# Earlier start of the first attention tile, earlier settling of two experts, and one pool of PSUM banks, in a recurrent-attention and top-1 router kernel

## The chip, the core and the metric

The kernel runs on one core of one Trainium2 chip. The metric is the device time of one execution in microseconds (us), lower is better. The core has five engines that run their own instruction streams in order: PE (TensorE, matmuls and transposes, with its weight loads shown as PEld), DVE (VectorE), ACT (ScalarE), POOL (GpSimd) and SP (SyncE, which here issues most of the DMA transfers). A stream waits for another through semaphores, and an instruction that waits holds up everything behind it on its engine.

## The reference

The first part is a linear recurrence over a sequence, for 4 batches, 8 heads, 768 steps, 48 values a head. The second part is a router that sends each of the 3072 rows to one of 8 experts of two matmuls each.

```python
for t in range(S):                       # B, H, S, D = 4, 8, 768, 48
    cur = einsum('bhd,bhe->bhde', u * k_t, v_t)          # a step's own term
    y[:, :, t] = einsum('bhd,bhde->bhe', r_t, state + cur)
    state = w * state + einsum('bhd,bhe->bhde', k_t, v_t)
x = y as 3072 rows of 384
xn, en = x / |x|, expert_emb / |expert_emb|
logits = xn @ en.T / tau                 # 8 experts
e = argmax(logits); gate = softmax(logits)[e]
out[row] = gate * (relu(x[row] @ w1[e]) @ w2[e])         # w1 384x1024, w2 1024x384
```

All arithmetic is float32.

## The kernel before

**Attention.** The sequence is cut into 6 chunks of 128 steps. A unit is one chunk of one batch, so there are 24 units, taken batch by batch within a chunk, and the function `attention` runs one turn for each, `i` from -1 to 23. The order of all instructions is written out by hand (`tc.manual_schedule()`), and the engines take them in that order. Turn `i` finishes unit `i` and prepares those after it:

- `load` (L262) fetches K, R and V of a unit in three transfers of 192 KB; turn `i` asks for unit `i+5`.
- `scaled` (L283) multiplies K by powers of the decay, and `own` (L287) computes u*K*R, a unit's own term. Both are on POOL; three instructions a unit. `own_sum` (L297, DVE) adds the own term up to eight numbers a step, `diag`, and `own_rows` (L303, ACT) multiplies V with them.
- `turn_r` and `turn_k` (L316, L327) transpose R and K on PE; their results are taken out of PSUM by DVE (`RT`) and ACT (`KT`). `scores` (L338) multiplies them, `masked` (L349, DVE) takes the scores out and cuts them to a triangle, in two halves `AT`, and `sums` (L382) multiplies these with V. `rows` (L416) turns the result into rows X, and `put` (L611, SP) writes them to DRAM as `xs`.
- every fourth turn the steps of the router run for the chunk that is complete: `logits`, `choose`, `before`, `ranks`, `places`, `exps`, `gates`, `lanes`, `listed`, `taken`, `summed`. They choose an expert for each row and build lists of which row takes which place at its expert.

`build_first` (L48) is the prologue: it computes the powers of the decay and prepares unit 0 up to its transposes. `build_consts` (L111) comes after it and makes masks and counters on POOL, and starts the ACT queue's loads of `u` (repeated over 128 partitions, 192 KB), `expert_emb`, `tau` and `w`. In turn -1 the own terms of units 0 and 1 are both computed, behind the scaling of unit 1. Three PE transposes of the expert embeddings (`build_experts`, L209) come at the top of turn 3, and some constants for the lists (`build_turned`, L169, DVE) at the end of turn 2.

**Two experts settled ahead.** After four of the six chunks, `settle` (L716) ranks the experts by the rows they have so far and settles which two are last in rank. Their first 128 rows each are then known, so that these two tiles (`Early`, L935) can be computed while the last two chunks are still being ranked. With `j = i - 12`:

```python
if j == 9:                                     # turn 21, before sums
    settle(k, load_, count)                    # DVE
    load_weights(k, expert_number(k, LAST[0]), k.weights[0])   # SP: w1, w2
    perm = turner(k, k.by)                     # DVE
if j == 10:                                    # turn 22, before sums
    k.lists = turned_lists(k, perm, "st")      # PE
    lists = taken_by_rank(k, k.lists)          # DVE
    first = [Early(k, r, *lists, w) for r, w in zip(LAST, k.weights)]   # POOL gathers
```

An expert's weights are 3 MB in two transfers. After the loop comes a passage written out by hand that ranks the last chunk and has the `Early` matmuls between its steps (`fill`).

**Experts.** `experts` (L1304) then runs eight blocks, one for each expert in the order `TURN`; each gathers its rows from `xs`, turns them (L1104), multiplies them with both weights, and scatters the result to `out` (L1020).

**PSUM.** It holds eight banks, and each tile here fills at most one. The attention part has a pool `aps` with two banks for each of the tags `tp`, `at` and `y` and one each for `st` and `xp`; this is closed at the end of the attention part, and the experts open a pool `ps` of eight.

Of the kernel before, what the change touches and what calls it, by code (L numbers as in the profile page):

```python
# [25 lines left out]
NK = DM // 128  # L26
# [21 lines left out]
def build_first(k):  # L48


    nc, pool = k.nc, k.aconst
    wc = pool.tile([128, NP], F32, name="wc")
    nc.vector.memset(wc, 1.0)
    with nc.allow_non_contiguous_dma(reason="384 words"):
        for s, q in ((0, nc.sync), (1, nc.scalar)):
            q.dma_start(out=wc[s * DP : s * DP + D, :], in_=k.w.rearrange("(p s) d -> s d p", s=2)[s])
    k.ones = k.const.tile([128, 128], F32, name="ones")
    nc.vector.memset(k.ones, 1.0)
    wide = k.work.tile([128, 512], F32, name="wide", tag="AT1")
    nc.vector.memset(wide, 1.0)  # L60
    k.ident = k.const.tile([128, 128], F32, name="ident")
    make_identity(nc, k.ident)

    ps = k.ps.tile([128, 512], F32, name="wake", tag="tp")
    for _ in range(WAKE):
        nc.tensor.matmul(ps, k.ones, wide, start=True, stop=True)
    for lst, name, count in ((k.Kpad, "Kpad", 4), (k.Rpad, "Rpad", AHEAD + 2)):
        for i in range(count):
            t = pool.tile([128, H, DP], F32, name=f"{name}{i}")
            nc.gpsimd.memset(t[:, :, D:DP], 0.0)  # L70
            lst.append(t)
    load(k, 0, nc.scalar)


    nc.vector.tensor_scalar(wc, wc, W_MIN, W_MAX, ALU.max, ALU.min)
    t = pool.tile([128, NP, C], F32, name="wpow")
    for p in range(NP):
        nc.vector.tensor_tensor_scan(
            t[:, p, :], wc[:, p : p + 1].to_broadcast([128, C]), k.ones, 1.0, ALU.mult, ALU.mult
        )  # L80
    mid = pool.tile([128, NP], F32, name="mid")
    nc.vector.reciprocal(mid, t[:, :, C // 2])
    over_i = mid[:, :, None].to_broadcast([128, NP, C])
    kp = k.work.tile([128, NP, C], F32, name="kp", tag="AT0")
    nc.vector.tensor_mul(kp, t[:, :, ::-1], over_i)
    ps = k.ps.tile([128, NP, 2, DP], F32, name="kpT", tag="xp")
    for p in range(NP):
        nc.tensor.transpose(ps[:, p].rearrange("q s d -> q (s d)"), kp[:, p, :], k.ident)
    k.rpow = pool.tile([128, NP, C], F32, name="rpow")
    nc.vector.tensor_mul(k.rpow, t, over_i)  # L90
    cols = ps[:, :, :, 0:D]
    nc.vector.tensor_mul(
        k.Kpad[0].rearrange("q (p s) d -> q p s d", s=2)[:, :, :, 0:D],
        k.loaded[0][0].rearrange("q (p s) d -> q p s d", s=2), cols,
    )
    turn_r(k, 0)
    k.kpow = pool.tile([128, H, D], F32, name="kpow")
    nc.vector.tensor_copy(k.kpow.rearrange("q (p s) d -> q p s d", s=2), cols)  # L98
    turn_k(k, 0)
    k.wC = t[:, :, C - 1 : C].to_broadcast([128, NP, D])  # L100
# [7 lines left out]
    return f  # L108


def build_consts(k):  # L111
    nc, pool = k.nc, k.const

    k.umask = pool.tile([128, 128], F32, name="umask")
    nc.gpsimd.memset(k.umask, 0.0)
    nc.gpsimd.affine_select(
        out=k.umask, in_=k.umask, compare_op=ALU.is_ge, fill=1.0,
        base=0, pattern=[[-1, 128]], channel_multiplier=1,
    )
    k.u_bc = k.aconst.tile([128, H, D], F32, name="u_bc")  # L120
    nc.scalar.dma_start(
        out=k.u_bc.rearrange("p h d -> p (h d)"),
# [7 lines left out]
    )  # L130
    k.wrow = k.aconst.tile([1, DM], F32, name="wrow")
    nc.scalar.dma_start(out=k.wrow, in_=k.w.rearrange("(o h) d -> o (h d)", o=1))
    k.yT = [k.aconst.tile([128, 2, NP // 2, C], F32, name=f"yT{i}") for i in range(2)]
    for b in range(B):
        t = k.aconst.tile([128, NP, D], F32, name=f"state{b}")
        nc.gpsimd.memset(t, 0.0)
        k.state.append(t)
    k.half = pool.tile([128, B], F32, name="half")
    nc.gpsimd.memset(k.half, 0.5)

# [68 lines left out]
def build_experts(k):  # L209

    nc, pool = k.nc, k.aconst
    emb, tau = k.emb_rows, k.tau_rows
    sq = k.work.tile([E, DM], F32, name="emb_sq", tag="sq")
    nrm = pool.tile([E, 1], F32, name="emb_nrm")
    nc.scalar.activation(sq, emb, ACT.Square, accum_out=nrm)
    nc.gpsimd.tensor_tensor(out=nrm, in0=nrm, in1=k.half[0:E, 0:1], op=ALU.pow)
    yield
    nc.vector.tensor_scalar_add(nrm, nrm, 1e-6)
    nc.vector.reciprocal(nrm, nrm)
    nc.vector.reciprocal(tau, tau)  # L220
    nc.vector.tensor_scalar(emb, emb, nrm, tau, ALU.mult, ALU.mult)
    yield
    ps = k.ps.tile([128, NK, E], F32, name="ps", tag="xp")
    for c in range(NK):
        nc.tensor.transpose(ps[:, c, :], emb[:, c * 128 : (c + 1) * 128], k.ident[0:E, 0:E])
    k.ent = k.const.tile([128, NK, 32], F32, name="ent")
    nc.vector.memset(k.ent, 0.0)
    nc.vector.tensor_copy(k.ent[:, :, 0:E], ps)
    yield

# [573 lines left out]
def attention(k):  # L804
# [17 lines left out]
    for i in range(-1, units):  # L822
        j = i - SETTLED * B
        if 0 < i + AHEAD < units:
            load(k, i + AHEAD)
        if 1 <= i < 4:
            next(emb)
        whole(summed, i - 6)
        whole(places, i - 4)
        whole(logits_out, i - 3)  # L830
        if i >= 0:
            on(turn_r, i + 1)
        if i < units - 1:
            on(own_rows, i, 0)
        if i >= 0:
            on(turn_k, i + 1)
        whole(turn_logits, i - 3)
        on(scaled, i + 2)
        for n in (0, 1) if i < 0 else (i + 2,):
            on(own, n)  # L840
        on(states, i)
        of_group(squares, i - 1)
        if i < units - 1:
            on(own_rows, i, 1)
        whole(norms, i - 2)
        whole(choose, i - 3)
        whole(before, i - 3)
        whole(located, i - 4)
        whole(gates, i - 5)
        whole(lanes, i - 5)  # L850
        whole(listed, i - 5)
        on(own_sum, i + 1)
        if j == 9:
            settle(k, load_, count)
            load_weights(k, expert_number(k, LAST[0]), k.weights[0])
            perm = turner(k, k.by)
        if i == units - 2:
            own_rows_once(k, i + 1)
        if j == 10:
            k.lists = turned_lists(k, perm, "st")  # L860
            lists = taken_by_rank(k, k.lists)
            first = [Early(k, r, *lists, w) for r, w in zip(LAST, k.weights)]
        on(sums, i)
        whole(exps, i - 4)
        on(carry, i)
        on(scores, i + 1)
        on(masked, i + 1, 0)
        on(rows, i)
        on(masked, i + 1, 1)
        of_group(put, i)  # L870
        of_group(turn_rows, i - 1)
        whole(logits, i - 2)
        whole(ranks, i - 3)
        whole(taken, i - 5)
        if i == B:
            decays(k)
        if i == 2:
            build_turned(k)
        if 3 <= i < 3 + len(k.ring):
            k.nc.gpsimd.memset(k.ring[i - 3], 0.0)  # L880
        if j == 7:
            load_, count = loads(k, "st")
        if j == 10:
            to = outs(k, lists[0], E * TM)

# [28 lines left out]
    exps(k, h)  # L914
    located(k, h)
    lanes(k, h)
    summed(k, g)
    by = order(k, load_, k.settled)
    perm = turner(k, by)
    gates(k, h)  # L920
    listed(k, h)
    fill(6)
    taken(k, h, "tp")
    summed(k, h)
# [508 lines left out]
def attention_pools(k, ctx):  # L1433
    for name, bufs in (("work", 2), ("rows", 3), ("rt", 2)):
        setattr(k, name, ctx.enter_context(k.tc.tile_pool(name=name, bufs=bufs)))
    k.ps = Banks(ctx.enter_context(k.tc.tile_pool(name="aps", bufs=1, space=PSUM)))


class Banks:


    def __init__(self, pool):
        self.pool = pool

    def tile(self, shape, dtype, name, tag):
        return self.pool.tile(shape, dtype, name=name, tag=tag, bufs={"tp": 2, "at": 2, "y": 2}.get(tag, 1))


def expert_pools(k, ctx):
    for name, bufs in (("gp", 8), ("xtp", 2), ("hp", 2)):  # L1450
        setattr(k, name, ctx.enter_context(k.tc.tile_pool(name=name, bufs=bufs)))
    k.ps = ctx.enter_context(k.tc.tile_pool(name="ps", bufs=8, space=PSUM))


@with_exitstack
def kernel(
# [23 lines left out]

    n.const = pool("const", 1)
    n.wp = pool("wp", 2)
    n.xs = tc.dram_tile([N, DM], F32, name="xs")
    n.list = tc.dram_tile([E, 128, TT], I32, name="list")
    n.tlist = tc.dram_tile([E, 128, TT], I32, name="tlist")
# [8 lines left out]
    with ExitStack() as ctx2, ExitStack() as ctx1, tc.manual_schedule():  # L1494
# [1 line left out]
        n.io = ctx1.enter_context(tc.tile_pool(name="io", bufs=AHEAD + 2))  # L1496
        attention_pools(n, ctx1)
        build_first(n)
        for i in range(1, AHEAD - 1):
            load(n, i)  # L1500
        build_consts(n)
        attention(n)
        ctx1.close()
        expert_pools(n, ctx2)
# [32 lines left out]
```

## Time and profile before

The time before is 424.53 us, the median of three runs from 424.11 to 425.92. The profiled execution has a span of 423.8 us.

| stage | us from the start | what bounds it in the profile |
|---|---|---|
| prologue and turn -1 | 0 to 12.3 | a chain over DVE, PE and POOL |
| wait of PE | 12.3 to 16.6 | no matmul runs |
| turns 0 to 23 | 16.6 to 146.7 | PE, with few gaps |
| wait of PE | 146.7 to 149.5 | no matmul runs |
| passage by hand | 149.5 to 178.2 | PE |
| experts | 178.2 to 412 | PE |
| last scatters | 412 to 423.8 | no matmul runs |

PE is busy for 398.1 us, DVE 251.6, ACT 171.4 and POOL 160.0. The transfers' queues move 54.39 MB. To read it: a gap on an engine other than PE matters only where PE waits for what comes behind it.

### The profile page before, as it was taken

The page shows a single profiled execution, that of the slowest core. Times are in us where ns is not written, and L with a number is a line of the kernel's source. Part 1 is how long each engine was busy: PE and PEld are TensorE (multiplying, and loading weights), DVE is VectorE, ACT ScalarE, POOL GpSimd, SP SyncE. Part 2 cuts the span into 40 slices and gives each one's busy share as a digit, 9 for nine tenths or more (in the row PEclk, how much of TensorE's full clock was granted, in tenths as well). Part 3 has the DMA queues.
Part 4 walks back from the last instruction along what each step waited for, and adds up shares of the span by engine and source line. Part 5 has one row for each costly group of instructions (what it writes and reads, how often), then busy time and mean ns, then how long its engine had stood idle before and what let it go on. Part 6 is the DMA issues. An engine that isn't in the chain of part 4 may idle for free.

```text
span 423.8 us, 9269 instructions
## 1 busy us (share of the span) xinstructions
PE 398.1 (94%) x3542; PEld 355.1 (84%) x3542; DVE 251.6 (59%) x608; ACT 171.4 (40%) x517; POOL 160.0 (38%) x217
## 2 busy tenths in 40 slices
PE   7599999999999789999999999999999999999980
PEld 4477888888888676689999999999999999799680
DVE  5377886867679755066765857175456456566310
ACT  1567776767677511233333233223233233223020
POOL 6777678686855215140140511140240240300210
PEclk9889999999999989999999999999999999999996
DMA  9977757666741982124643614164164160140101
GB/s 151 195 157 152 151 130 148 133 144 131 149 94 45 360 322 57 39 76 157 225 160 131 224 37 148 49 217 151 37 226 148 39 223 2 44 162 1 56 20 43
DMA packets 93800, 54.39 MB, mean 128 GB/s; under 512 B 76937, under 2 KB 88380, under 8 KB 93746
## 3 DMA queue, kind: packets, MB, share of 16 engines
q1 hardware_dynamic: 89024, 43.85, 38.9%
q0 software_dynamic: 3296, 9.44, 6.7%
q10 hardware_dynamic: 1426, 0.41, 0.5%
q8 instruction: 30, 0.49, 0.5%
q14 instruction: 24, 0.20, 0.2%
HBM read 44.45 MB, written 9.63 MB: 128 GB/s over the span
## 4 chain that ended last, share of the span: by engine, by line
PE 80%; POOL 6%; DMA 5%; issue 3%; DVE 2%; SPq 2%; ACT 0%; POOLq 0%; ACTq 0%
PE ps L1156 24%; PE ps L1220 15%; PE ps L1260 5%; PE at L345 4%; PE y L406 4%; PE ps L1273 4%; PE ps L1134 2%; PE ps L1104 2%; PE early_y L975 2%; PE y L397 2%; PE kt L333 2%; PE early_h L966 2%; PE st L366 2%; PE yrows L424 2%; PE rt L322 2%
## 5 line engine op out<-in xcount | busy, mean ns | idle before, releaser
L1020 POOL DMA_INDIRECT out_dram<-y,to x25 | 29.8, 1193 | 176.4 <-issue 118.6
L1156 PE MATMUL ps<-xTe,w 128*128 128x192 f32 (+3 forms) x336 | 63.0, 327 | 0.0
L1156 PEld LDWEIGHTS ps<-xTe,w 128*128 128x128 f32 x336 | 55.8, 190 | 0.6 <-ACT p L1170 0.2
L308 ACT ACTIVATE xd<-V,diag 128x48 f32<-128x48 f32 x184 | 46.2, 325 | 3.2 <-DVE diag L299 3.2
L351 DVE TENSOR_TENSOR AT<-at,umask 128x512 f32<-128x512 f32 x48 | 32.9, 686 | 22.1 <-PE at L345 22.1
L1163 ACT ACTIVATE hT<-hT 128x384 f32<-128x384 f32 (+3 forms) x42 | 21.9, 523 | 33.8 <-DVE hT L1186 15.4
L1220 PE MATMUL ps<-Tw,Sh 128*128 128x192 f32 x192 | 32.5, 326 | 0.0
L1220 PEld LDWEIGHTS ps<-Tw,Sh 128*128 128x128 f32 x192 | 31.4, 190 | 0.0
L406 PE MATMUL y<-AT,V 128*48 128x128 f32 (+1 forms) x384 | 26.9, 281 | 4.4 <-DVE AT L351 4.4
L345 PE MATMUL at<-RT,KT 48*128 48x128 f32 x384 | 28.8, 291 | 1.3 <-ACT KT L335 0.7
L1011 POOL DMA_INDIRECT G<-xs,take x25 | 26.2, 1048 | 9.8 <-issue 4.6
L1156 PE MATMUL ps<-Tx,Sw 128*128 128x192 f32 (+3 forms) x168 | 29.8, 327 | 0.0
L345 PEld LDWEIGHTS at<-RT,KT 48*128 48x128 f32 x384 | 24.1, 193 | 5.9 <-ACT xd L308 2.8
L1173 DVE TENSOR_TENSOR u<-ps,p 128x384 f32<-128x384 f32 (+3 forms) x14 | 7.8, 558 | 35.4 <-PE ps L1156 30.7
L1156 PEld LDWEIGHTS ps<-Tx,Sw 128*128 128x128 f32 x168 | 27.6, 190 | 0.2 <-DVE Tx L1287 0.2
L406 PEld LDWEIGHTS y<-AT,V 128*48 128x48 f32 (+1 forms) x384 | 20.5, 125 | 8.1 <-DVE AT L351 4.7
L512 ACT COPY xT<-xp 128x384 f32<-128x384 f32 x24 | 11.5, 478 | 34.1 <-PE xp L510 34.1
L292 POOL TENSOR_TENSOR KU<-K,u_bc 128x384 f32<-128x384 f32 x24 | 24.1, 1003 | 3.1 <-DMA K<-in_k_dram 3.1
L293 POOL TENSOR_TENSOR KU<-KU,Rpad 128x384 f32<-128x384 f32 x24 | 24.1, 1003 | 1.9
L284 POOL TENSOR_TENSOR Kpad<-K,kpow 128x384 f32<-128x384 f32 x23 | 23.0, 1001 | 2.9 <-DVE kpow L98 2.9
L1220 PE MATMUL ps<-w,hT 128*128 128x192 f32 x128 | 23.4, 326 | 0.0
L1220 PEld LDWEIGHTS ps<-w,hT 128*128 128x128 f32 x128 | 21.3, 190 | 0.3
(239 smaller groups left out, 806.0 us busy)
## 6 DMA issues: line engine op xcount, KB each, us to landing
w<-in_moe_w_dram SPq DMA_DIRECT2D x16, 1536.0 KB, 7.6
K<-in_k_dram SPq DMA_DIRECT2D x24, 192.0 KB, 3.0
V<-in_v_dram SPq DMA_DIRECT2D x24, 192.0 KB
xs<-X SPq DMA_DIRECT2D x24, 192.0 KB, 13.0
Rpad<-in_r_dram SPq DMA_DIRECT2D x23, 192.0 KB, 5.8
G<-xs,take POOLq DMA_INDIRECT x27
out_dram<-y,to POOLq DMA_INDIRECT x25
Rpad<-in_r_dram ACTq DMA_DIRECT2D x1, 192.0 KB
```

What stands on the lines that cost most here:

```text
L284: k.nc.gpsimd.tensor_mul(k.Kpad[i % len(k.Kpad)][:, :, 0:D], k.loaded[i][0], k.kpow)
L292: nc.gpsimd.tensor_mul(KU, K, k.u_bc)
L293: nc.gpsimd.tensor_mul(KU, KU, R[:, :, 0:D])
L308: k.nc.scalar.mul(k.xd[i][:, h, :], V[:, h, :], diag[:, h : h + 1])
L345: nc.tensor.matmul(at[s][:, p, :], KT[rows, p, :], RT[rows, p, :], start=True, stop=True)
L351: k.nc.vector.tensor_mul(a, k.at[i][s], k.umask[:, None, :].to_broadcast([128, NP, C]))
L406: mm(y[s][u * DP : u * DP + n, q, :], V[:, h * D : h * D + n], AT[s][:, p, :], start=(c == 0 and q == 0), stop=True, skip_group_check=True,)
L1011: nc.gpsimd.indirect_dma_start(out=G[0:n, :], out_offset=None, in_=k.xs[:, :], in_offset=IndirectOffsetOnAxis(ap=take[0:n], axis=0), bound ...
L1020: put = k.nc.gpsimd.indirect_dma_start(out=k.out[:, :], out_offset=IndirectOffsetOnAxis(ap=to, axis=0), in_=y, in_offset=None, bounds_chec ...
L1156: nc.tensor.matmul(ps[:, j, :], weights[:, (f + j) * 128 : (f + j + 1) * 128], moving, start=(first and j == 0), stop=True, skip_group_che ...
L1163: nc.scalar.activation(h, h, ACT.Relu)
L1220: nc.tensor.matmul(ps, a[:, f, :], b[:, f, :], start=(first and f == 0), stop=(f == NF // 2 - 1), skip_group_check=True)
```

## The change

The change has three parts. The first brings what unit 0's mask step waits for ahead: the small loads go out at the start on the ACT queue, the constants follow at once on POOL, and unit 0's own term is computed in the prologue. In turn 0 the second half of `own_rows` goes ahead of `turn_k`; the embedding's steps move behind `own_sum`, `build_turned` from turn 2 to turn 5, and the zeroing of `ent` from DVE to POOL. The second settles the two experts a turn sooner, with the gathers put ahead of the second weight transfer, and in the passage by hand it brings the last chunk's `gates` and `listed` ahead of the ordering. The third replaces both PSUM pools by one with eight named banks, of which each tag has its own and the experts' tag goes round all eight.

```diff
 build_first:
     load(k, 0, nc.scalar)
+    load(k, 1)
+    load_consts(k)          # u_bc, emb, tau, wrow on the ACT queue
+    build_consts(k)
+    for i in range(2, AHEAD - 1):
+        load(k, i)
+    own(k, 0)
 build_consts:
+    k.ent = pool.tile([128, NK, 32], F32, name="ent")
+    nc.gpsimd.memset(k.ent, 0.0)
 attention:
-        if 1 <= i < 4:
-            next(emb)
         whole(summed, i - 6)
...
+        if i == 0:
+            own_rows(k, i, 1)
         if i >= 0:
             on(turn_k, i + 1)
...
-        for n in (0, 1) if i < 0 else (i + 2,):
-            on(own, n)
+        on(own, i + 2)
...
-        if i < units - 1:
+        if 0 < i < units - 1:
             on(own_rows, i, 1)
...
         on(own_sum, i + 1)
-        if j == 9:
-            settle(k, load_, count)
-            load_weights(k, expert_number(k, LAST[0]), k.weights[0])
-            perm = turner(k, k.by)
+        if 1 <= i < 4:
+            next(emb)
+        if j == 7:
+            load_, count = loads(k, "xp")
         if i == units - 2:
             own_rows_once(k, i + 1)
-        if j == 10:
+        if j == 9:
+            perm = turner(k, k.by)
             k.lists = turned_lists(k, perm, "st")
             lists = taken_by_rank(k, k.lists)
             first = [Early(k, r, *lists, w) for r, w in zip(LAST, k.weights)]
+            load_w2(k, number, k.weights[0][1])
         on(sums, i)
...
-        if i == 2:
+        if i == B + 1:
             build_turned(k)
...
-        if j == 7:
-            load_, count = loads(k, "st")
+        if j == 8:
+            settle(k, load_, count)
+            number = expert_number(k, LAST[0])
+            load_w1(k, number, k.weights[0][0])
         if j == 10:
             to = outs(k, lists[0], E * TM)
 the passage by hand:
     lanes(k, h)
+    gates(k, h)
+    listed(k, h)
     summed(k, g)
     by = order(k, load_, k.settled)
     perm = turner(k, by)
-    gates(k, h)
-    listed(k, h)
     fill(6)
 PSUM:
-    k.ps = Banks(ctx.enter_context(k.tc.tile_pool(name="aps", bufs=1, space=PSUM)))
-    k.ps = ctx.enter_context(k.tc.tile_pool(name="ps", bufs=8, space=PSUM))
+    HELD = {"tp": (0, 1), "at": (2, 3), "y": (4, 5), "st": (6,), "xp": (7,), "ps": (0, 1, 6, 7, 2, 3, 4, 5)}
+    n.ps = Banks(pool("psum", 1, space=PSUM))
```

More of the change, by code (lines that the diff above doesn't have):

```diff
@@ L108, in numbers, with load_consts @@
     return f
[L111 to L119, printed above, removed]
+def load_consts(k):
+    nc = k.nc
     k.u_bc = k.aconst.tile([128, H, D], F32, name="u_bc")
@@ L132, in build_consts @@
     nc.scalar.dma_start(out=k.wrow, in_=k.w.rearrange("(o h) d -> o (h d)", o=1))
+def build_consts(k):
+    nc, pool = k.nc, k.const
+    k.umask = pool.tile([128, 128], F32, name="umask")
+    nc.gpsimd.memset(k.umask, 0.0)
+    nc.gpsimd.affine_select(
+        out=k.umask, in_=k.umask, compare_op=ALU.is_ge, fill=1.0,
+        base=0, pattern=[[-1, 128]], channel_multiplier=1,
+    )
     k.yT = [k.aconst.tile([128, 2, NP // 2, C], F32, name=f"yT{i}") for i in range(2)]
@@ L225, in build_experts @@
         nc.tensor.transpose(ps[:, c, :], emb[:, c * 128 : (c + 1) * 128], k.ident[0:E, 0:E])
-    k.ent = k.const.tile([128, NK, 32], F32, name="ent")
-    nc.vector.memset(k.ent, 0.0)
     nc.vector.tensor_copy(k.ent[:, :, 0:E], ps)
@@ L1435, in attention_pools @@
         setattr(k, name, ctx.enter_context(k.tc.tile_pool(name=name, bufs=bufs)))
-    k.ps = Banks(ctx.enter_context(k.tc.tile_pool(name="aps", bufs=1, space=PSUM)))
 class Banks:
+    HELD = {"tp": (0, 1), "at": (2, 3), "y": (4, 5), "st": (6,), "xp": (7,), "ps": (0, 1, 6, 7, 2, 3, 4, 5)}
     def __init__(self, pool):
         self.pool = pool
+        self.next = {tag: itertools.cycle(banks) for tag, banks in self.HELD.items()}
     def tile(self, shape, dtype, name, tag):
-        return self.pool.tile(shape, dtype, name=name, tag=tag, bufs={"tp": 2, "at": 2, "y": 2}.get(tag, 1))
+        return self.pool.tile(shape, dtype, name=name, tag=f"bank{next(self.next[tag])}")
 def expert_pools(k, ctx):
@@ L1498 @@
         build_first(n)
-        for i in range(1, AHEAD - 1):
-            load(n, i)
-        build_consts(n)
         attention(n)
```

## The prediction, made before the changed kernel had run

> **What bounds the kernel now.** I read the page first, then the waits of PE, the timeline of the first 42 us, the granted clock in short windows, and the timeline from 126 to 182 us.
>
> ```profile
> PE 398.1 (94%) x3542; PEld 355.1 (84%) x3542; DVE 251.6 (59%) x608; ACT 171.4 (40%) x517; POOL 160.0 (38%) x217
> PE   7599999999999789999999999999999999999980
> PEclk9889999999999989999999999999999999999996
> ```
>
> PE is busy for 94% of the span, so only its own gaps and slow spells can be won back. They lie in slices 0 to 2 and 13 to 14 (a slice is 10.6 us). The waits of PE name them (total, times, longest, in us):
>
> ```profile
> PE y L406 <- DVE AT L351: 4.4, 1, 4.4
> PE early_x L955 <- DMA G<-xs,take: 2.8, 1, 2.8
> ...
> PE ps L1104 <- ACT earlyy L978: 0.7, 1, 0.7
> ...
> PE at L345 <- ACT xd L308: 0.6, 1, 0.6
> PE ps L225 <- ACT xT L512: 0.6, 1, 0.6
> PE take L672 <- POOL what L653: 0.5, 1, 0.5
> ```
>
> Each of the six is touched by this change. The timeline of the start (start, length in us, engine, line, instruction) shows the first:
>
> ```profile
> 8.84 0.35 ACTq L121 DMA_DIRECT2D u_bc<-in_u_dram  x1
> ...
> 9.24 1.00 POOL L284 TENSOR_TENSOR Kpad<-K,kpow 128x384 f32<-128x384 f32 x1 [2.91 <-DVE kpow L98]
> ...
> 13.35 0.99 POOL L292 TENSOR_TENSOR KU<-K,u_bc 128x384 f32<-128x384 f32 x1 [3.11 <-DMA K<-in_k_dram]
> 14.41 0.99 POOL L293 TENSOR_TENSOR KU<-KU,Rpad 128x384 f32<-128x384 f32 x1
> ...
> 15.44 0.55 DVE L299 TENSOR_REDUCE diag<-KU 128x8 f32<-128x384 f32 x1 [6.28 <-POOL KU L293]
> 15.91 1.28 DVE L351 TENSOR_TENSOR AT<-at,umask 128x512 f32<-128x512 f32 x2
> ```
>
> The scores of unit 0 are ready at 10.6, but the mask L351 stands on DVE behind the sum L299, and this waits for the own term, which POOL begins at 13.35. The page puts that on K; but K of unit 0 had already been read at 7.53, so I take it for `u_bc`, sent at 8.84 behind the copy of KT on ACT.
>
> A wait costs a second time. Busy time in windows (PE, PEld, DVE, ACT, POOL, granted clock, DMA share, GB/s):
>
> ```profile
> 12.30:16.60 4.30, 0.00 (x0) 0.00 (x0) 1.16 (x3) 1.07 (x7) 3.10 (x4) 1.00 1.03 203
> ...
> 17.20:24.00 6.80, 6.80 (x56) 5.54 (x55) 4.21 (x8) 3.85 (x15) 6.64 (x9) 0.50 0.90 175
> 146.80:149.50 2.70, 0.00 (x0) 0.00 (x0) 0.70 (x4) 0.44 (x1) 0.00 (x0) 1.00 0.95 337
> ...
> 150.20:153.70 3.50, 3.50 (x35) 2.71 (x34) 1.81 (x4) 1.26 (x4) 1.10 (x3) 0.51 0.98 393
> ```
>
> After the wait of 4.3 us PE runs at half clock for 6.8 us, and after that of 2.8 us for 3.5. Sixteen `scores` matmuls take 2.08 us at 18.29 and 1.16 at 24.97.
>
> **What the Trainium skill says.** "TensorE: Matmul & The Clock Gate", Part 1, says that PE's clock is halved after an idle window of about 3.4 us, restored after a busy one, and that the windows run freely. The trace agrees: the half-clock spells last one and two windows (3.5 and 6.8). It also shows that the window need not be wholly idle, for 2.8 us sufficed. The same page, Part 2 (architectural detail), has DVE, ACT and POOL as strict first-in first-out, as the mask behind the sum shows. "Trainium Kernel Development and Optimization", Key Constraints, says that the transfers of the SP, ACT and POOL queues share 16 engines; here 203 GB/s moved while `u_bc` was on its way.
>
> **The start.** With `load_consts` in the prologue, `u_bc` goes out behind R of unit 0 on the ACT queue, at about 1.9 us. By the windows 0.3 MB had moved at 4.0 and 0.93 MB at 6.9 us; K, R and V of unit 0 and `u_bc` are 0.79 MB, so it lands at about 6.2. As a bound, in the trace of before it took 4.5 us (8.84 to 13.35), which gives 6.4. POOL ends its constants at 6.33, and the zeroing of `ent` adds some 0.15. The own term of unit 0 then runs from 6.5 to 8.5 (2 x 1.00), in an interval where POOL idled until 9.24. The sum L299 follows `kpow` at 9.16 and ends at 9.7, before the scores at 10.6, so the masks run from 10.6 to 11.9. PE reaches `sums` of unit 0 at 12.2 and does not wait: **-4.4 us**. No mostly idle window remains, so the half clock of 6.8 us goes too: half of 6.8, **-3.4**.
>
> Do the later steps keep pace? POOL, at 3.6 us a turn, has scaled unit 2 by 13.2, and PE wants it at 15.3. Doing 8 `own_rows` ahead of KT(1) costs ACT 2.0 us from 9.75, and KT(1) is out at 12.3, wanted at 13.2. Units 0 to 5 and `u_bc` are 3.7 MB, at 185 GB/s in by about 21.6; unit 5 is wanted on POOL in turn 3 at 23. After that a turn needs 0.77 MB, 3.9 us at 197 GB/s, against 4.7 or more of PE. So transfers hide, with 2 us to spare at unit 5. One loss: the square of the embeddings (0.5 + 0.2 us) now stands on ACT in turn 1 behind the second half of `own_rows` and ahead of the copy of y that `rows` needs: between 0 and 0.7, I take **+0.5**.
>
> **Turn 3.** The embedding's transposes waited 0.57 for the bank `xp`, and the scores waited 0.59 (35.63) because DVE had `build_turned` and the `ent` steps (2.2 us) ahead of RT. Moved behind `states`, the first goes. In turn 6, where `build_turned`'s 1.95 us now fall, PE has 3.4 us of work between the rows and the scores instead of 2.5, since the state matmuls (0.65) are there; DVE needs 2.6 for constants and RT. So the second goes as well: **-1.2**.
>
> **Settling a turn sooner.** What it removes is the wait for the gather: **-2.8**, and the half clock behind it, **-1.7** (half of 3.5). What it adds is a wait of PE in turn 21. In the trace of before the DVE steps stand without a gap: the second mask ends at 132.73, then `summed`, RT, `own_sum`, `settle` (134.09 to 135.9) and `turner`, and `perm` is ready at 136.27. The new order holds the same instructions, with `settle` first. But the list matmul, which in turn 22 found `perm` long ready, now stands on PE in turn 21 right before `sums`, where PE arrives at 133.35. Behind it on PE is everything: `sums`, the next scores, the masks on DVE that need them. So PE waits **+2.9** (136.27 - 133.35). If that falls into one free-running window, the clock halves once more: 0 or 1.7, I take the middle, **+0.85**.
>
> The gather itself then has room. It starts near 137.5 instead of 142.59, and took 6.9 us with both weights in transfer; so it is there at about 145 on the old time axis, while PE reaches `early_x` at 146.7 + 2.9 = 149.6. That the first weights go out 1.5 us sooner changes nothing, for their first use was at 152.5. The second expert's go out some 3 us later and are wanted at 166.5, with 3 MB at 390 GB/s taking 8. So the wait moves from turn 23 to turn 21 and the part nets **-0.75**.
>
> **The passage by hand.** With `gates` ahead of the ordering, `what` L653 comes over 1 us sooner, and PE's 0.54 before `take` goes: **-0.5**. The ordering comes later, but it is hidden by `early_y`.
>
> **One PSUM pool.** The experts' first tile now takes bank 0, idle by then, instead of waiting until the last `early_y` is out of its pool: **-0.7**. Within each part the rotation over banks is as before, two for each of three tags and eight for `ps`; nothing for it. The expert phase and the last 12 us, where POOL scatters, keep their length.
>
> Sum: -4.4 - 3.4 + 0.5 - 1.2 - 0.75 - 0.5 - 0.7 = -10.4, so 424.5 - 10.4 = **414.1 us**.
>
> **Rivals.**
> - *The list wait isn't there.* If DVE had slack that the trace hides, the new wait and its clock share fall away: 414.1 - 3.75 = 410.3. Against it: DVE stands without a gap from 132.65 to 137.9.
> - *The start gives part back to the transfers.* If u_bc or the loads of units 2 to 5 come some 2 to 4 us later than reckoned, PE waits in turns 1 to 3, and a half-clock window can follow: about 3.4 less gained, 417.5. For it: from 4 to 22 us the DMA share is near 1.
> - *Slower.* `own` of unit 0 now stands on POOL ahead of the scaling of unit 1, which PE's KT(1) needs before `sums` of unit 0. If `u_bc` lands at 13.3 again, that costs about 0.9 and wins nothing at the start; if the gather is also late as before, the transition costs 2.9 + 0.85 more. With -1.2 - 0.5 - 0.7 this is 424.5 + 2.3 = 426.8. Against it: `u_bc` now has only R ahead of it in its queue, where before the loads of units 2 and 3 were in transfer with it.
>
> **How the numbers follow.** Forecast 0.60, no list wait 0.11, part given back 0.17, slower 0.06, and 0.06 for losses of several parts at once that leave it near no change. The range takes the forecast with its unknown terms (clock after the list wait 0 to 1.7, `emb` 0 to 0.7, `u_bc` by 1 us), most of the second rival and the edge of the first: 410.5 to 419. Half a per cent is 2.1 us: faster 0.88, within 0.06, slower 0.06.
>
> **What would show it.** Right: PE's first `y` L406 near 12.2, granted clock 1.0 through 24 us, own term on POOL at 6.5 to 8.5; a PE wait of about 3 us at the list matmul, released by DVE `perm`; no wait at `early_x`; no wait at the first L1104. Wrong: `u_bc` after 8 us, PE waits for loads before 30 us, a gather still awaited near the end of the loop, or any change of the span from the first L1104 to the end (245.5 us now).

## The result, and the profile after

The changed kernel takes 420.38 us (median of four runs, 419.49 to 420.78), the kernel before 424.77 beside it (424.11 to 425.92): a ratio of 0.9891 with a 95% interval of 0.9863 to 0.9919. That is 4.4 us less where 10.4 were forecast, and the time lies above the range of 410.5 to 419. The profiled span went from 423.8 to 418.9 us.

The page of the changed kernel, in busy time and in 40 slices (10.5 us each):

```profile
PE 397.3 (95%) x3542; PEld 355.0 (85%) x3542; DVE 254.4 (61%) x607; ACT 172.3 (41%) x517; POOL 161.2 (38%) x218
PE   6999999999996999999999999999999999999980
PEclk9899999999997999999999999999999999999996
```

PE's busy time hardly fell, 398.1 to 397.3. A half clock makes busy time longer, so had the half-clock spells of before gone (10.3 us of them, 5.1 us of loss), busy time would be some 5 us less. It is 0.8 less: 4.1 of the 4.9 us came out of idle time. Counting from 0, two slices of the clock line, besides the last, where PE has nothing left to do, show where full clock was still missing: slice 1, where the start was to have none left, and slice 12.

The waits of PE of the changed kernel (total, times, longest, in us):

```profile
PE lists L772 <- DVE perm L766: 3.3, 1, 3.3
...
PE kpT L94 <- DVE kp L91: 1.0, 1, 1.0
PE kt L343 <- DVE Kpad L98: 0.7, 1, 0.7
...
PE kt L343 <- DVE X L440: 0.4, 1, 0.4
PE yrows L434 <- ACT yT L421: 0.3, 1, 0.3
...
PE take L682 <- POOL what L663: 0.2, 1, 0.2
```

Gone are the waits for the first mask (4.4), at `early_x` (2.8), at the experts' first bank (0.7) and both of turn 3; that before `take` is 0.2 instead of 0.5. The list matmul waits 3.3, where 2.9 had been foretold. So the list of waits looks as forecast, but for two of the prologue: 1.0 at `kpT`, which is new, and 0.7 instead of 0.2 for `Kpad`. The windows tell the rest (PE, PEld, DVE, ACT, POOL, granted clock, DMA share, GB/s); two of them overlap:

```profile
11.20:14.50 3.30, 3.30 (x33) 2.97 (x35) 2.70 (x5) 1.51 (x6) 3.22 (x4) 0.51 1.41 196
14.50:24.00 9.50, 8.76 (x123) 7.29 (x121) 5.74 (x11) 6.37 (x23) 7.60 (x10) 0.99 1.08 197
...
128.70:132.00 3.30, 0.00 (x0) 0.03 (x1) 2.98 (x14) 2.00 (x7) 1.39 (x2) 0.81 0.15 24
131.00:137.50 6.50, 5.50 (x50) 4.50 (x50) 1.30 (x8) 0.75 (x2) 2.29 (x2) 0.50 0.83 297
137.50:142.00 4.50, 4.50 (x76) 3.58 (x74) 3.72 (x12) 3.16 (x12) 0.00 (x0) 0.99 1.08 379
```

The wait for the lists is idle PE from 128.7 to 132.0. Behind it the clock stays at a half until 137.5; PE worked 5.5 us in that time. If all of that work went at half speed, half of it, 2.7 us, is loss; this is an estimate, and so is each loss below that is half of PE's work in a spell. There is a spell at a half from 11.2 to 14.5 as well, worth 1.65.

A third view puts a date on each loss: the start of the `scores` of a unit, and of the experts' first transposes (L1104, now L1117). "Again" is another profile of the same changed kernel.

| start, us | before | changed | again |
|---|---|---|---|
| scores of unit 0 | 9.47 | 10.03 | 9.69 |
| unit 1 | 18.29 | 15.22 | 13.28 |
| unit 4 | 35.63 | 29.82 | 27.91 |
| unit 7 | 52.21 | 46.40 | 44.49 |
| unit 8 | 57.63 | 52.57 | 50.66 |
| unit 20 | 125.13 | 120.38 | 118.47 |
| unit 21 | 129.79 | 125.04 | 123.13 |
| first expert transposes | 178.25 | 173.64 | 170.74 |
| end of the span | 423.8 | 418.9 | 416.6 |

By unit 4 the changed kernel is 5.81 us ahead (7.72 again); by unit 8, 5.06 (6.97); by unit 21, 4.75 (6.66). From unit 21 to the experts before took 48.46, changed 48.60 (47.61 again): the settling, the hand passage and the pool together won nothing, or 0.85. The experts take as long as before (245.3 after 245.5).

### The profile page after: what moved, and what is told of

Same layout as the page of the kernel before. It is cut to its first block, busy times and chain, and to the rows that moved or that the text cites. A ratio compares the mean times of both kernels' runs of the same rounds, so it can differ in the third digit from the quotient of the medians.

```text
span 418.9 us, 9283 instructions
## 1 busy us (share of the span) xinstructions
PE 397.3 (95%) x3542; PEld 355.0 (85%) x3542; DVE 254.4 (61%) x607; ACT 172.3 (41%) x517; POOL 161.2 (38%) x218
## 4 chain that ended last, share of the span: by engine, by line
PE 82%; DVE 5%; POOL 4%; issue 3%; DMA 1%; ACT 1%; POOLq 0%; SPq 0%; DVEq 0%; ACTq 0%
PE ps L1169 24%; PE ps L1233 16%; PE ps L1273 5%; PE at L355 5%; PE y L416 5%; PE ps L1286 4%; PE early_y L988 3%; PE ps L1147 2%; PE early_h L979 2%; PE kt L343 2%; PE ps L1117 2%; PE y L407 2%; PE yrows L434 2%; PE st L376 2%; PE rt L332 2%
## 5 line engine op out<-in xcount | busy, mean ns | idle before, releaser
L1024 POOL DMA_INDIRECT G<-xs,take x25 | 26.7, 1067 | 10.5 <-issue 4.3
L1196 ACT ACTIVATE hT<-ps 128x384 f32<-128x384 f32 (+3 forms) x14 | 6.9, 491 | 36.0 <-PE ps L1169 36.0
```

What stands on the lines that cost most here:

```text
L1024: nc.gpsimd.indirect_dma_start(out=G[0:n, :], out_offset=None, in_=k.xs[:, :], in_offset=IndirectOffsetOnAxis(ap=take[0:n], axis=0), bound ...
```

## The experiments

Four questions were open: what the settling is worth and why, what the parts of the start are worth, whether the pool matters, and where a better order lies. Times are medians of four to seven runs, and ratios are to the kernel before, run beside. In the edits some lines are drawn together, and `...` marks lines left out. "The transition" is the stretch from the scores of unit 21 to the first expert transposes.

**The changed kernel as a control.** It was run again beside the second batch.

> The changed kernel unchanged, beside the others on one chip, for its spread. Theory: the half-clock spell at the start (11.1 to 14.5 us in its profile) depends on where the free-running windows fall and need not come in each execution, so the mean clock lies between 0.976 and 0.985 and the times between 418.5 and 421.5. Rival: the spell belongs to the new prologue, and all executions have a mean clock of 0.976 to 0.980 and lie within 1 us.

419.25 us (417.81 to 421.34, six runs), ratio 0.9858 (0.9827 to 0.9889). The six spread over 3.5 us, in step with the mean granted clock: 417.81 at 0.985, 421.34 at 0.976. Its profile has no half clock at the start and one window behind the lists:

```profile
11.20:14.50 3.30, 3.30 (x56) 2.84 (x54) 2.31 (x6) 2.64 (x10) 3.14 (x5) 1.00 1.22 198
...
130.00:133.60 3.60, 3.51 (x36) 2.71 (x36) 0.48 (x3) 0.37 (x1) 1.87 (x2) 0.53 0.89 308
```

So the half-clock spells of this kernel vary between executions. The one at the start is the rarer: of the eleven profiles with the new prologue, two of them with a part of it altered, only that of the change has it.

**All but the earlier settling.** The settling, its weights and its lists stand where they stood before.

```diff
-        if j == 7: load_, count = loads(k, "xp")     # mid-turn
         if j == 9:
+            settle(k, load_, count)
+            load_weights(k, expert_number(k, LAST[0]), k.weights[0])
             perm = turner(k, k.by)
+        if j == 10:
             k.lists = turned_lists(k, perm, "st")
             lists = taken_by_rank(k, k.lists)
             first = [...]
-            load_w2(k, number, k.weights[0][1])
...
-        if j == 8: settle(...); load_w1(...)         # end of turn
+        if j == 7: load_, count = loads(k, "st")
```

> The changed kernel with the settling, the list step and the first weights put back to turns 19, 21 and 22 as before; the early start, the order by hand at the end and the pool stay changed. Theory: the earlier settling loses more at the list wait than it wins at the gather (6.1 us lost by the scores of unit 23, 4.5 won back behind it), so without it the time is 1.5 to 2 us lower, about 418.5; the wait at early_x is back at 2 to 3 us with a half-clock window behind it. Rival: the earlier settling pays and its absence costs 1 to 4 us, 421 to 424.

416.8 us, ratio 0.9808 (0.9786 to 0.983): faster than with the earlier settling, and by more than expected. The waits of PE of this kernel and its windows show the old cost back in full:

```profile
PE early_x L966 <- DMA G<-xs,take: 3.8, 1, 3.8
```

```profile
139.00:141.00 2.00, 0.00 (x0) 0.00 (x0) 0.45 (x4) 0.19 (x1) 0.00 (x0) 1.00 1.05 399
...
143.00:145.00 2.00, 2.00 (x31) 1.60 (x28) 1.81 (x4) 0.99 (x3) 0.00 (x0) 0.62 1.02 408
145.00:147.00 2.00, 2.00 (x12) 1.46 (x7) 0.11 (x1) 0.27 (x1) 1.75 (x3) 0.52 1.02 401
```

A wait of 3.8 and a window at half clock, and still the transition takes 47.17 here, less than the changed kernel's 48.60 and 47.61. Against the 48.46 of before, the hand passage and the pool give 1.29 net (forecast 1.2). Up to `early_x` nothing is won: PE reaches it 0.9 sooner after unit 21, since a wait of 0.9 for `yT` is gone, and waits there 1.0 longer. From `early_x` to the first expert transposes it takes 27.32, and took 28.73 before.

**The earlier settling alone, in the kernel before.**

```diff
         # kernel before
+        if j == 7: load_, count = loads(k, "xp")
         if j == 9:                                   # turn 21
-            settle(k, load_, count)
-            load_weights(k, expert_number(k, LAST[0]), k.weights[0])
             perm = turner(k, k.by)
-        if j == 10:
             k.lists = turned_lists(k, perm, "st")
             ...
+            load_w2(k, number, k.weights[0][1])
-        if j == 7: load_, count = loads(k, "st")
+        if j == 8: settle(...); load_w1(...)         # end of turn 20
```

> The kernel before with the earlier settling alone: loads in turn 19, settle and the first weights at the end of turn 20, list matmul, gathers and second weights in turn 21 ahead of sums. Theory: it exchanges a wait of 2.8 us and a half-clock spell of 3.5 us at early_x for a wait of 3.3 us and a spell of 3.4 to 6.8 us at the list matmul, so alone it makes the kernel slower by 0 to 3 us, about 425 to 428. Forecast as written: 0.75 us faster, 424.

428.51 us (426.44 to 430.0, seven runs), ratio 1.0061 (1.0037 to 1.0086): slower by itself. Two waits and four windows:

```profile
PE y L406 <- DVE AT L351: 4.7, 1, 4.7
PE lists L762 <- DVE perm L756: 3.3, 1, 3.3
```

```profile
135.00:137.00 2.00, 0.00 (x0) 0.00 (x0) 1.90 (x9) 1.43 (x7) 0.79 (x1) 1.00 0.00 0
...
139.00:141.00 2.00, 2.00 (x24) 1.52 (x18) 0.00 (x0) 0.37 (x1) 1.56 (x2) 0.50 1.02 416
...
145.00:147.00 2.00, 2.00 (x28) 1.55 (x25) 0.51 (x1) 1.01 (x4) 0.00 (x0) 0.50 1.06 373
147.00:149.00 2.00, 2.00 (x31) 1.66 (x31) 1.45 (x6) 1.60 (x7) 0.00 (x0) 0.88 0.58 196
```

The list wait is 3.3 again. From 139 to past 147 the clock is a half while PE is busy without a gap. In all, the spell lasts 10.2 us here, three windows of 3.4.

**The lists behind the turn's work.** The earlier settling stays; only the list matmul, what DVE makes of it and the gathers move to the end of turn 21.

```diff
         if j == 9:
             perm = turner(k, k.by)
-            k.lists = turned_lists(k, perm, "st")
-            lists = taken_by_rank(k, k.lists)
-            first = [...]
             load_w2(k, number, k.weights[0][1])
...
         of_group(turn_rows, i - 1)
+        if j == 9:
+            k.lists = turned_lists(k, perm, "st")
+            lists = taken_by_rank(k, k.lists)
+            first = [...]
```

> The changed kernel with the list matmul, the take tiles and the two gathers moved from ahead of sums to the end of turn 21, behind the masks and the rows. Theory: PE's wait for perm (3.3 us) and the half clock behind it (6.8 us at half speed, of which PE works 5.5, so 2.7 us) are what the earlier settling costs, and the gather has room to spare; then both go, the granted clock stays at 1.0 through turn 21, no wait at early_x appears, and the time falls by 6 us to about 414.4. Rival: the gather is only hidden because PE is held up by the list wait; then PE reaches early_x 6 us sooner and waits 2 to 3 us for it, with a half-clock window behind it, and the time is about 418 to 419.

415.13 us (414.55 to 415.34), ratio 0.9762 (0.9747 to 0.9778). The list wait is gone, `early_x` doesn't wait, and the clock stays full. The gathers fly beside both weight transfers and come in time. Two smaller waits are new:

```profile
PE lgT L536 <- DVE gates L779: 1.3, 1, 1.3
PE at L355 <- DVE RT L334: 0.9, 1, 0.9
```

So the place of the list matmul on PE cost the change its gain, not the settling's moment. Whether the settling had to be earlier at all, the next pair asks.

**Settled as before, lists at the end of turn 21.** `settle`, both weights and `turner` stand in turn 21 as in the kernel before, and the lists, in a bank of `y`, half a turn ahead of their old place. The second kernel has `build_turned` at the end of turn 3 in addition.

```diff
         on(own_sum, i + 1)
-        if j == 7: load_, count = loads(k, "xp")
         if j == 9:
+            settle(k, load_, count)
+            load_weights(k, expert_number(k, LAST[0]), k.weights[0])
             perm = turner(k, k.by)
-            (lists, gathers, load_w2)
...
         of_group(turn_rows, i - 1)
+        if j == 9:
+            k.lists = turned_lists(k, perm, "y")
+            lists = taken_by_rank(k, k.lists)
+            first = [...]
...
-        if j == 8: settle(...); load_w1(...)
+        if j == 7: load_, count = loads(k, "st")
-        if i == B + 1:          # second kernel only
+        if i == B - 1:
             build_turned(k)
```

> The changed kernel with settle, the first weights and turner back in turn 21 behind own_sum as before, but with the list matmul and the gathers at the end of turn 21 behind the rows, in a bank of tag y, instead of in turn 22 as before or ahead of sums as changed. Theory: perm is ready by then, so PE waits for nothing there, RT and the logits are not held up as in late_list (0.9 and 1.3 us), and the gather starts 4 us sooner than before, which takes away the wait of 3.8 us at early_x and its half clock of 3.4 us. Time 411.5 to 413. Rival: the gather's flight is set by the 3 MB of weights that are sent ahead of it and not by its start; then it lands at the same time, the wait stays near 3 us and the time near 416.

> As between, with build_turned at the end of turn 3 instead of turn 5. Theory: in turn 5 its 2 us on DVE run into choose and before of turn 6 and delay the masks, which cost 0.75 us between the scores of units 7 and 8; in turn 3 nothing is behind it, so that 0.75 us is won: about 411.5, and the scores of unit 8 stand 0.7 us closer to those of unit 7. Rival: PE is delayed there by the router's own steps whatever build_turned does, and nothing changes.

413.22 us (412.58 to 413.48, just above what was expected), ratio 0.9706 (0.9684 to 0.9728), and 412.66 (412.64 to 412.9), ratio 0.9696 (0.9675 to 0.9718): the best of the study, 3% below the kernel before. In the first of them the timeline and a window show why:

```profile
131.40 1.29 POOL L955 DMA_INDIRECT G<-xs,take  x1 [3.63 <-DVE gates L779]
```

```profile
135.00:140.00 5.00, 4.71 (x56) 3.69 (x56) 4.30 (x19) 2.46 (x8) 0.18 (x1) 1.00 1.04 374
```

The gather is issued at 131.40, and `early_x` starts at 138.7 without a wait for it, though both weights went out ahead of it and the DMA queues moved 374 GB/s. So it needed at most 7.3 us, and sending it ahead of the second weights was not needed. The transition is 42.66, 4.5 less than with the old settling. That is as much as the forecast put on the wait and the half clock that go (2.8 + 1.7), but its parts differ and offset each other. The wait that goes is 3.8. From `early_x` to the first expert transposes only 0.7 is won (26.62 after 27.32): the spell lengthens PE's work there by 1.1 (27.32 after 26.21), not by half of its 3.4, and without it PE waits 0.4 for others. As for `build_turned`, unit 7's scores to unit 8's take 5.42 with it at turn 3, against 6.18. But from unit 4 to unit 7 they take 17.22 against 16.58, so its net gain is about 0.1, and the 0.56 us between the two medians isn't explained by it.

**Idle matmuls ahead of the lists.** To tell PE's idleness from everything else in that stretch, matmuls that nobody reads fill the wait of the changed kernel; its order and transfers stay.

```diff
         if j == 9:
             perm = turner(k, k.by)
+            ps = k.ps.tile([128, 128], F32, name="warm", tag="y")
+            for _ in range(24):           # second kernel: 12
+                k.nc.tensor.matmul(ps, k.ones, k.ones, start=True, stop=True)
             k.lists = turned_lists(k, perm, "st")
```

> The changed kernel with 24 idle 128-column matmuls (0.11 us each at full clock, 2.6 us) on PE ahead of the list matmul, inside the wait for perm of 3.3 us. It removes no wait; it only keeps PE at work. Theory: the list wait costs twice, once as a wait and once as a half-clock spell behind it; with PE at work there is no spell, the granted clock stays at 1.0 from 125 to 140 us and the time falls by 1.7 to 2.7 us, to about 417. Rival: the slow stretch behind the wait is not due to the idle time of PE (the 3 MB of weights are in transfer just then), so it stays at half clock and the time is unchanged, about 419.5 to 420.

> The kernel with 24 idle matmuls ahead of the list matmul ran at full clock through the transition, but its fillers took 5.5 us where the gap is 3.3, so the lists came 2.0 us later than they could. Here 12 fillers stand there, 2.75 us at 0.229 us each: the lists should follow perm at once, PE's wait there be about 0.5 us, and the clock stay at 1.0. Theory (PE's idleness at the list matmul causes the half clock): no window at half clock from 125 to 150, scores of unit 21 to the first expert transposes about 45.9 us, time about 2 us below that of the kernel with 24 fillers, 415.8. Rival (the half clock comes from what runs in that stretch, and 24 fillers only moved it): a spell at 0.5 is back behind the lists, that distance is 47.6 or more, time 417.8 or above.

With 24: 417.84 us, ratio 0.9826 (0.9805 to 0.9848). The clock is full, but each filler took 0.23 (two records of it count as one), twice what I reckoned:

```profile
125.56 5.52 PE L872 MATMUL warm<-ones 128*128 128x128 f32 x48
```

So the lists came late, and the time was above the expected 417 or so. With 12: 416.1 us (415.54 to 416.63), ratio 0.9787 (0.9768 to 0.9805), where 415.8 was expected. Its waits and windows:

```profile
PE lists L772 <- DVE perm L766: 0.7, 1, 0.7
```

```profile
130.00:132.00 2.00, 2.00 (x40) 1.74 (x32) 0.11 (x2) 0.74 (x2) 1.38 (x2) 1.00 0.92 379
132.00:134.00 2.00, 2.00 (x39) 1.51 (x35) 1.72 (x3) 0.51 (x2) 0.91 (x1) 1.00 1.00 403
134.00:136.00 2.00, 2.00 (x33) 1.66 (x34) 1.40 (x6) 2.00 (x8) 0.00 (x0) 1.00 1.06 388
```

The fillers do no useful work, the transfers are at 379 to 403 GB/s, no less than in the changed kernel's half-clock spells (297 and 308), and the clock is 1.0. The transition takes 46.10 (expected 45.9), 1.5 and 2.5 less than the two profiles of the changed kernel. PE's idleness at the list matmul causes the half clock; the rival falls. Without fillers the same wait of 3.3 stands in six profiles, and each has a spell behind it, of one, two or three windows:

| kernel | half clock behind the list wait, us |
|---|---|
| changed | 6.8 |
| changed, again | 3.4 |
| two pools | 6.8 |
| own term late | 3.4 |
| fillers in the prologue | 10.2 |
| earlier settling alone | 10.2 |

**The two PSUM pools of before, and the own term in turn -1.** Two kernels undo one part each.

```diff
 # first kernel: pools "aps" and "ps" as before, in place of eight named banks
 # second kernel: the early loads stay
 build_first:
-    own(k, 0)
 attention:
-        on(own, i + 2)
+        for n in (0, 1) if i < 0 else (i + 2,):
+            on(own, n)
```

> The changed kernel with the two PSUM pools of before. Theory: the first transposes of the experts wait again for the last copy of early_y, 0.7 us, and nothing else differs, about 421.1. Rival: the pools make no difference that can be measured, 420.4.

> The changed kernel with unit 0's own term computed in turn -1 behind the scaling of unit 1, as before, while the small loads stay early. Theory: the own term on POOL beside rpow on DVE delays both (rpow 1.5 us instead of 0.7, the second half of the own term 1.3 instead of 1.0), so rpow is back at 0.7 and the scores of unit 0 come 0.5 us sooner; but the masks then wait for the own term until about 13, PE idles about 1 us more before sums of unit 0, and the time is 0 to 2 us higher than 420.4. If the early loads alone had done all the work, the time would be the same or lower.

Two pools: 421.32 us, ratio 0.9908 (0.9888 to 0.9929). The wait at the experts' first bank (0.7) is back; the times can't tell 0.7 us from the spread of this kernel. The stretch from `early_x` to the first expert transposes can, for it has full clock in these profiles: 26.63 in the changed kernel, 27.53 with two pools, and 28.13 with the old passage by hand as well (the earlier settling alone). So the pool is worth 0.9 and the passage 0.6. Own term late: 419.73 us, ratio 0.9878 (0.986 to 0.9895). No loss shows in the time, where 0 to 2 us were expected. The trace shows one:

```profile
PE y L415 <- DVE AT L360: 1.3, 1, 1.3
```

PE's first `y` waits 1.3 for the mask, not the 4.4 of before. So the early loads and constants did most of the work on that wait. The rest is worth more than 1.3: the scores of unit 4 start at 29.13, against 26.96 in the kernel with 12 fillers, though those of unit 0 start together (8.68 and 8.55). Why the time doesn't show these 2 us stays open; the spell behind the lists lasts one window in this profile and two in that of the change.

**Fillers in the prologue.** Four idle matmuls after each of unit 0's transposes were to remove the half clock from 11.2 to 14.5.

```diff
     turn_r(k, 0)
+    ps = k.ps.tile([128, 128], F32, name="warm", tag="y")
+    for _ in range(4): nc.tensor.matmul(ps, k.ones, k.ones, start=True, stop=True)
     turn_k(k, 0)
+    # the same four once more
```

> The changed kernel with four idle 128-column matmuls (0.1 us each) put on PE behind the transposes of R of unit 0, and four behind those of K, where PE waits 0.7 us each. Theory: the half clock at the start comes from a window with too little PE work in the prologue; then no window in the first 20 us is at half clock, at a cost of 0.5 us at most, and the times are 0.5 to 1.7 us lower than the changed kernel's beside it. Rival: the spell comes from something else, and it remains at unchanged or slightly longer times.

421.91 us, ratio 0.9889 (0.9858 to 0.9919): no gain, and the scores of unit 0 start at 10.47. There was no half clock at the start in its profile, but none in the control's either, so this tells nothing of what causes that spell. The profile's time is long for another reason: three windows at half clock behind the lists.

## Why the prediction was wrong

**The start, -4.4 - 3.4 + 0.5, and turn 3, -1.2.** Their sum, -8.5, should stand at unit 4. It is -5.81 in the changed kernel's profile, -7.72 again, and -8.67 in the kernel with 12 fillers, whose prologue is the same (35.63 - 26.96); five other profiles with this prologue give -7.9 to -8.9. So the mechanism was right and the whole sum can be had, but not in every execution. The step that failed here, in one profile of eight, reads "No mostly idle window remains, so the half clock of 6.8 us goes too". In the profile of the change a window from 11.2 to 14.5 was at half clock, 1.65 us. Another 0.3 to 1.5 us had been lost before it, since the scores of unit 0 began at 10.03, 9.69 and 8.55 in the three. Against the last of these it is DVE that was late: the clamp of the decay (L81) took 1.11 instead of 0.23 beside POOL's memsets, which stood there before too, and `rpow` 1.51 instead of 0.68 beside the own term that the change had put there. In the 3.4 us ahead of the spell PE was then busy for 2.0; in the 3.4 us from 7.3 of the other execution, for 2.5. This points to a window that was idle enough after all, but no run tests it. The wait for the loads that the second rival feared is nowhere. Turn 3 gave what was forecast: unit 3's scores to unit 4's shrank from 6.11 to 5.04. What decides on the half clock at 11.2 stays open.

**`build_turned`, costed at nothing.** I reckoned that in turn 6 PE has 3.4 us of other work. PE indeed doesn't wait for RT there. But DVE then runs without a gap from 43.3 to 49, so the masks of that turn start when DVE gets to them. From unit 7's scores to unit 8's it takes 6.17 instead of 5.42: +0.75, in every profile of the changed kernel. I followed the delay to its first reader on PE and not to the next. With `build_turned` at the end of turn 3 the 5.42 is back, but most of it is lost again between units 4 and 7.

**The settling, -0.75.** This is the step that failed most. On record: "-2.8", "-1.7", "+2.9", and "0 or 1.7, I take the middle, +0.85". What it removes came out at 4.5, as the kernel with the lists at the end of turn 21 shows, though partly by luck: the wait in its comparison was 3.8 and the half clock cost 0.7. What it adds was mis-sized. The wait was 3.3. The half clock behind it cost 1.65 or 2.75, not 0.85: no profile with this wait was without a spell, which I had given even odds, and four of six had two or three windows, which I hadn't reckoned with. And the new place of `loads` costs 0.3: unit 8's scores to unit 20's take 67.8 with it and 67.5 without. So the term is -4.5 + 3.3 + 2.75 + 0.3 = +1.85 in the profile of the change, not -0.75. Against the kernel with the old settling it measures 48.60 - 47.17 + 0.3 = +1.73, and +0.74 again. By itself it made the kernel before 3.0 us slower.

**The hand passage and the pool, -0.5 - 0.7.** Right in mechanism and nearly in size: -0.6 and -0.9 in the stretch behind `early_x`, 1.29 net where a spell is in both.

Together on the span, 10.4 - 4.9 = 5.5 us are missing: 2.7 at the start, 0.75 at `build_turned` and 2.5 at the settling make 5.95, less some tenths won in the rest. The likeliest rival in the forecast was a loss to the transfers, and it didn't happen. The loss was to the granted clock, which I took as one coin toss of 1.7 us in one place. One reference of the forecast is to be put right: what it takes from the Trainium skill, "TensorE: Matmul & The Clock Gate", on the strict order of DVE, ACT and POOL stands in Part 1, under "Architectural detail", and not in Part 2.

## What to carry to other kernels

In these kernels an idle stretch of PE of about 3 us cost its length and then up to half of a spell at half clock of 3.4 to 10.2 us behind it. So a wait that is moved, not removed, should be priced with more than one window, and a kernel that has such waits should be timed over many executions. If the wait must stay, matmuls that nobody reads can fill it: 12 of them brought the ratio from 0.9891 and 0.9858 down to 0.9787. Where one small matmul needs a long chain on another engine, put it behind the work that PE already has, even if its result is wanted early. Follow a delayed engine past the first reader that still gets its data in time.

## What the runs showed of the hardware

The shared path of DVE and POOL took more than expected. The Trainium skill, "SBUF — State Buffer", section "SBUF: two separate sides", says that some DVE operations and all of POOL's share a port pair that one of them holds for a whole instruction while the other is fully blocked. The traces fit this. In the profile of the change, on DVE and then on POOL:

```profile
6.68 1.51 DVE L96 TENSOR_TENSOR rpow<-wpow,mid 128x512 f32<-128x512 f32 x1
...
128.41 0.68 DVE L732 TENSOR_SCALAR settled<-by 128x8 f32<-128x8 f32 x1
```

```profile
128.07 1.00 POOL L303 TENSOR_TENSOR KU<-KU,Rpad 128x384 f32<-128x384 f32 x1
```

`settled`, of 8 numbers a partition, takes 0.17 in turn 21 of the kernel before. At its new place it takes 0.67 to 0.70 in all nine profiles that have it there, and in this one it ends as POOL's instruction does; those 0.5 us are about what the list wait exceeded the forecast by. `rpow` took 0.69 in the kernel before and 1.51 here, where unit 0's own term on POOL began 0.05 ahead of it. In the kernel with the lists behind the turn's work `rpow` began first, and POOL's instruction was the longer one, 1.44 instead of 1.00:

```profile
6.67 0.68 DVE L96 TENSOR_TENSOR rpow<-wpow,mid 128x512 f32<-128x512 f32 x1
```

```profile
6.78 1.44 POOL L302 TENSOR_TENSOR KU<-K,u_bc 128x384 f32<-128x384 f32 x1 [0.34 <-DMA u_bc<-in_u_dram]
```

Where the own term began after `rpow` had ended, `rpow` took 0.68 or 0.69. No run was made to separate the two engines, so this is a reading of the traces and not an experiment.

The half clock also outlasted its cause by more than one window: from 139 to past 147 us PE was busy without a gap and at a half, in the kernel with the earlier settling alone. Shorter waits of PE had no spell behind them: 1.3 and 0.9 in the kernel with the lists behind the turn's work, 1.3 in the one with the late own term. The kernels without an idle stretch at the lists or at `early_x` ran at a mean clock of about 0.99 and spread by 1.1 us at most over their runs; the changed kernel and the settling alone ran at 0.971 to 0.985 and spread by 3.5 and 3.6, though the kernel with the late own term, which has the list wait too, spread by 0.8 over its four runs. And a filler matmul of 128 columns took 0.23 us in two records, where I had counted one of 0.11.
